# Smaller loads, a joint output step and shared evictions in the opening of an attention-and-MLP kernel

## The chip, the cores and the metric

One Trainium2 chip, one of its cores. The metric is the device time of one execution in microseconds (us). Three runs of the kernel before stand below. The profile is one further execution, whose own time and span are given beside it.

## The reference

Two parts are chained. The first is a decayed linear attention over batch 4, 8 heads, 768 positions and head size 64, in blocks of 64 positions with a running 64 by 64 state per batch and head. The second is an MLP without bias on all 3072 tokens: 512 to 2048, a quick GELU, 2048 to 512.

```
intra = einsum('bhic,bhjc->bhij', qb, kb) * Dmask          # lam**(i-j), i >= j
intra = einsum('bhij,bhjd->bhid', intra, vb)
inter = einsum('bhid,bhde->bhie', qb * lam_pow, kv_state)
out[:, :, sl] = intra + inter
kv_state = lam_block * kv_state + einsum('bhsd,bhse->bhde', kb * rev_pow, vb)
...
h = x @ w_in                                               # x: 3072 x 512, heads side by side
g = h * (1.0 / (1.0 + np.exp(-1.702 * h)))
return g @ w_out
```

Inputs and output are float32; the kernel multiplies in bfloat16 and accumulates in float32.

## The kernel before, in words

The 3072 tokens are worked in six waves of 512. Waves 0 and 1 are the first 256 positions of two batches each (the "big" form); waves 2 to 5 take 128 positions of all four batches. Heads go in four pairs; pair p holds heads 2p and 2p+1. The MLP of a wave begins once the attention output x of all four pairs is there: `mlp1` makes 16 tiles of 512 columns, each of four accumulating steps kc 0 to 3, and kc p reads x of pair p. `mlp2` makes four output tiles of 16 steps each.

The order of every instruction on every engine is written out by hand (`manual_schedule`), and an engine works in that order. Wave 0's attention is a straight list of calls in the opening. The attention of wave w + 1 is slipped between the MLP's items of wave w: `BIG` lists for wave 1 at which item each step is placed, and `EARLY = 3` is the number of `mlp1` tiles that are begun on pairs 0 and 1 before the output step of pairs 2 and 3.

The steps of the big form, for one pair p:

- `big_cast` (L225) multiplies k or q by powers of lam into `kqb`, one instruction per batch, on VectorE (`V`) or GpSimd (`G_`). `big_cast_v` (L229) casts v on GpSimd.
- `big_t` (L238) transposes k and q on TensorE into PSUM and evicts them to `kqB`: ACT (L242), or for q VectorE (L240).
- `big_s` (L255) makes the scores in two PSUM banks, `big_m` (L262) masks and scales them on VectorE into `sm`, a tile with six buffers.
- `big_kv` (L279) makes the products of k and v of two pairs for both halves of the 256 positions. ACT copies the first half into `mid` (L283) and into `first` (L284). `big_st` (L291) joins the halves into the state `kv` for wave 2, on VectorE.
- `big_c` (L299, L307) makes the output of one pair from `mid`, v and the masked scores. Two PSUM banks are evicted to x (L311), by ACT or by VectorE.

`fill` (L217) puts matmuls on zeros into the order, which write a bank that the next step overwrites. PSUM banks come from two pools: five for attention, three for transposes of wave 0 and for the MLP.

Loads of q, k and v are issued by SP (the first two of q by ACT). The weights `w_in` (five column tiles) and `w_out` (four) are issued by GpSimd (L176, L180), in between its casts. A small load that reads w_out (`sync_behind_weights`, L188) holds SP's next loads, those of wave 1, back until a part of the weights has landed.

## Time and profile before

| what | value |
|---|---|
| runs | 304.63, 215.71, 215.8 us; median 215.8 |
| profiled execution | 215.14 us, span 213.4 us |
| granted TensorE clock | 0.999 |
| TensorE (PE) busy | 204.8 us, 96% of the span |
| VectorE (DVE) busy | 83.8 us, 39% |
| ScalarE (ACT) busy | 87.4 us, 41% |
| GpSimd (POOL) busy | 33.2 us, 16% |
| DMA | 33.83 MB, 159 GB/s over the span |

A busy time is the sum of the engine's instruction durations without overlap. A large share says that the engine is nearly always at work; where the idle rest lies must be read from stretches of the span. In rows of the timeline and of the chain of waits the first number is the start and the second the length, both in us; square brackets hold the idle time before a group and what ended it.

### The profile page before, as it was taken

The page shows a single profiled execution, that of the slowest core. Times are in us where ns is not written, and L with a number is a line of the kernel's source. Part 1 is how long each engine was busy: PE and PEld are TensorE (multiplying, and loading weights), DVE is VectorE, ACT ScalarE, POOL GpSimd, SP SyncE. Part 2 cuts the span into 40 slices and gives each one's busy share as a digit, 9 for nine tenths or more (in the row PEclk, how much of TensorE's full clock was granted, in tenths as well). Part 3 has the DMA queues.
Part 4 walks back from the last instruction along what each step waited for, and adds up shares of the span by engine and source line. Part 5 has one row for each costly group of instructions (what it writes and reads, how often), then busy time and mean ns, then how long its engine had stood idle before and what let it go on. Part 6 is the DMA issues. An engine that isn't in the chain of part 4 may idle for free.

```text
span 213.4 us, 4323 instructions
## 1 busy us (share of the span) xinstructions
PE 204.8 (96%) x1757; PEld 101.1 (47%) x1757; DVE 83.8 (39%) x186; ACT 87.4 (41%) x164; POOL 33.2 (16%) x62
## 2 busy tenths in 40 slices
PE   7779999999999999999999999999999999999994
PEld 2454444545444455444545444545444545444453
DVE  3687100285751573624272624272624071100121
ACT  4683673445666122366302366302376302466000
POOL 4599000562130012101110001120000000000000
PEclk9999999999999999999999999999999999999999
DMA  5999999999899989699981399981390012100112
GB/s 137 268 248 198 203 197 248 295 267 200 186 276 213 198 190 229 221 188 223 221 195 52 114 184 223 227 191 56 114 178 0 3 51 94 53 2 0 49 49 98
DMA packets 88839, 33.83 MB, mean 159 GB/s; under 512 B 68724, under 2 KB 85876, under 8 KB 88820
## 3 DMA queue, kind: packets, MB, share of 16 engines
q1 hardware_dynamic: 83524, 29.11, 57.9%
q0 software_dynamic: 4752, 4.19, 12.5%
q10 hardware_dynamic: 544, 0.26, 0.5%
q8 instruction: 13, 0.21, 0.4%
q14 instruction: 6, 0.05, 0.1%
HBM read 27.27 MB, written 6.29 MB: 157 GB/s over the span
## 4 chain that ended last, share of the span: by engine, by line
PE 91%; DMA 4%; DVE 1%; ACT 1%; POOL 1%; SPq 0%; issue 0%; POOLq 0%
PE ps_h L378 39%; PE ps_out L391 38%; DMA vb<-in_v_dram 2%; PE ps_o L362 2%; PE ps_o L355 2%; PE ps_s L321 2%; PE ps_part L402 2%; DMA qb<-in_q_dram 2%; PE ps_o L307 1%; PE ps_s L255 1%; PE ps_kv L279 1%; PE ps_kv L338 1%; ACT xT L311 1%; PE ps_tq L238 1%; ACT g_sb L381 1%; POOL vb L229 1%
## 5 line engine op out<-in xcount | busy, mean ns | idle before, releaser
L378 PE MATMUL ps_h<-xT,w_in 128*128 128x512 bf16 x384 | 85.3, 379 | 1.1 <-ACT xT L311 0.5
L391 PE MATMUL ps_out<-w_out,g_sb 128*128 128x512 bf16 x368 | 83.7, 379 | 0.0
L381 ACT ACTIVATE g_sb<-ps_h 128x512 bf16<-128x512 f32 x96 | 56.9, 597 | 44.9 <-PE ps_h L378 44.6
L378 PEld LDWEIGHTS <-w_in 128*128 128x128 bf16 x384 | 37.0, 98 | 45.5 <-issue 1.6
L391 PEld LDWEIGHTS <-g_sb 128*128 128x128 bf16 x368 | 34.5, 98 | 40.2
L325 DVE SCALAR_TENSOR_TENSOR sm<-ps_s,inv_pow,mask 128x512 bf16<-128x512 f32 x32 | 21.8, 744 | 28.6 <-PE ps_s L321 28.6
L395 DVE COPY o_sb<-ps_out 128x512 f32<-128x512 f32 x19 | 13.1, 691 | 47.0 <-PE ps_out L391 46.6
L367 ACT CAST xT<-ps_o 128x512 bf16<-128x512 f32 x16 | 8.6, 589 | 44.4 <-PE ps_o L362 44.4
L202 POOL CAST v_sb<-vf 128x512 bf16<-128x512 f32 x16 | 10.4, 652 | 84.8 <-DMA vf<-in_v_dram 84.8
L225 DVE TENSOR_TENSOR kqb<-kb,kb_pow 128x256 bf16<-128x256 f32 x14 | 6.3, 492 | 19.7 <-DMA kb<-in_k_dram 17.1
L262 DVE SCALAR_TENSOR_TENSOR smb<-ps_s,inv_pow,mask_b 128x512 bf16<-128x512 f32 x16 | 11.0, 745 | 5.9 <-PE ps_s L255 4.8
L345 DVE SCALAR_TENSOR_TENSOR kv<-kv,blk_pow,ps_kv 128x256 bf16<-128x256 bf16 x12 | 5.2, 478 | 17.2 <-PE ps_kv L338 17.2
L200 DVE TENSOR_SCALAR kqs<-qf,q_pow 128x256 bf16<-128x256 f32 x32 | 11.1, 348 | 0.6 <-DMA qf<-in_q_dram 0.6
L225 POOL TENSOR_TENSOR kqb<-qb,qb_pow 128x256 bf16<-128x256 f32 x12 | 7.8, 663 | 22.0 <-DMA qb<-in_q_dram 19.7
L199 DVE TENSOR_SCALAR kqs<-kf,k_pow 128x256 bf16<-128x256 f32 x32 | 11.1, 347 | 0.0
L395 ACT COPY o_sb<-ps_out 128x512 f32<-128x512 f32 x4 | 2.3, 585 | 10.4 <-PE ps_out L391 10.4
L242 ACT COPY kqB<-ps_tk 128x512 bf16<-128x512 bf16 x8 | 4.6, 594 | 2.5 <-PE ps_tk L238 2.4
L238 PEld LDWEIGHTS <-kqb 128*128 128x128 bf16 x64 | 3.9, 98 | 3.6 <-DVE kqb L225 1.3
L355 PEld LDWEIGHTS <-kv 64*64 64x64 bf16 x128 | 3.8, 106 | 3.4 <-issue 3.4
L217 PE MATMUL fill<-warm 128*128 128x512 bf16 x10 | 4.0, 584 | 1.3 <-DVE i_blk L135 1.3
L321 PEld LDWEIGHTS <-kqT 64*128 64x128 bf16 x128 | 3.6, 94 | 3.4 <-issue 3.4
L229 POOL CAST vb<-vb 128x512 bf16<-128x512 f32 x8 | 4.7, 616 | 3.3 <-DMA vb<-in_v_dram 3.2
(61 smaller groups left out, 99.5 us busy)
## 6 DMA issues: line engine op xcount, KB each, us to landing
out_dram<-o_sb SPq DMA_DIRECT2D x23, 256.0 KB, 2.0
kf<-in_k_dram SPq DMA_DIRECT2D x32, 128.0 KB, 3.3
qf<-in_q_dram SPq DMA_DIRECT2D x32, 128.0 KB, 3.5
vf<-in_v_dram SPq DMA_DIRECT2D x32, 128.0 KB, 3.4
vb<-in_v_dram SPq DMA_DIRECT2D x8, 256.0 KB, 5.2
w_out<-in_moe_w_out_dram POOLq DMA_DIRECT2D x4, 512.0 KB, 14.2
kb<-in_k_dram SPq DMA_DIRECT2D x6, 256.0 KB, 5.5
qb<-in_q_dram SPq DMA_DIRECT2D x6, 256.0 KB, 5.9
```

The lines of the kernel that those rows point to most:

```text
L199: nc.vector.tensor_scalar(ks[:, :, h, :], kf[:, :, h, :], scalar1=k_pow[:, hd : hd + 1], scalar2=None, op0=MUL)
L200: nc.vector.tensor_scalar(qs[:, :, h, :], qf[:, :, h, :], scalar1=q_pow[:, hd : hd + 1], scalar2=None, op0=MUL)
L202: nc.gpsimd.tensor_copy(v_sb[w % 2][p], vf)
L225: eng.tensor_tensor(x[:, bb].rearrange("p t (h d) -> p h t d", h=2), pair_of(w, nm, p)[:, bb], by, op=MUL)
L262: nc.vector.scalar_tensor_tensor(sm.rearrange("p b t s -> p b (t s)"), s2.rearrange("p b t s -> p b (t s)"), inv_pow[:, 2 * p + h : 2 * p ...
L325: nc.vector.scalar_tensor_tensor(sm, s2[p, h], inv_pow[:, 2 * p + h : 2 * p + h + 1], mask.to_broadcast([P, B, P]), op0=MUL, op1=MUL)
L355: nc.tensor.matmul(ps_o[p][hs, b, :], kv_sb[w % 2][p][hs, b, :], trans[w, p][hs, 1, b, :], start=(b == 0), stop=False, skip_group_check=True)
L367: nc.scalar.copy(x, ps_o[p].rearrange("p b s -> p (b s)"))
L378: nc.tensor.matmul(h_ps[fc], w_in_sb[j][:, kc, i * P : (i + 1) * P], xT[w, kc], start=(kc == 0), stop=(kc == KC - 1))
L381: nc.scalar.activation(g_of[w][:, fc, :], h_ps.pop(fc), GELU)
L391: nc.tensor.matmul(ps_out, g_of[w][:, fc, g * P : (g + 1) * P], w_out_sb[j][:, fc % CW, :], start=(fc == 0), stop=(fc == FFC - 1))
L395: (nc.scalar.copy if w == 0 else nc.vector.tensor_copy)(o, ps_out)
```

## The change

- Wave 0 loads k and q of pairs 2 and 3 pair by pair (k2, q2, k3, q3), 128 KB a load, where it loaded 256 KB for both; v of these pairs comes last, as before.
- `big_cast` takes one engine per batch: the q products of wave 0's pairs 1 to 3 are made half on GpSimd, half on VectorE.
- `big_t` can do k or q alone, so the transposes of pairs 2 and 3 are spread between other steps.
- `big_c` takes a tuple of pairs. Pairs 0 and 1 are one step with two PSUM banks and one copy per bank; x of two pairs is one tile. Each bank is evicted by its own engine, ACT and VectorE in most places; in wave 0 the joint step's copies are both on ACT and placed later (`big_x`).
- `big_parts` has ACT copy both halves of the k and v products to SBUF in float32 (`part`), and `big_st` joins them on GpSimd with two instructions per pair, after wave 0's weights have been issued.
- `sm` has eight buffers.
- `mlp1`'s early tiles run [0, 1] and then [2, 3], where they ran [0, 1], [2], [3].
- `BIG` is renumbered, with wave 1's transposes and scores of pairs 0, 1 one item later; other engines take some of its casts.
- The third and later w_in tiles move behind later casts on GpSimd, and the fillers of wave 0 are fewer.

```diff
-        for nm, h0 in (("v", 0), ("k", 4), ("q", 4), ("v", 4)):
-            load_big(0, nm, h0, 4, nc.sync)
+        load_big(0, "v", 0, 4, nc.sync)
+        for h0 in (4, 6):
+            for nm in "kq":
+                load_big(0, nm, h0, 2, nc.sync)
+        load_big(0, "v", 4, 4, nc.sync)
...
-    def big_cast(w, nm, p, eng):
+    def big_cast(w, nm, p, *engs):
...
-        for bb in range(BB):
+        for bb, eng in enumerate(engs if len(engs) == BB else engs * BB):
...
-        for h in range(2):
+        for h, eng in enumerate(engs):
             hs = slice(64 * h, 64 * h + 64)
-            nc.scalar.copy(mid_sb[p0 // 2][hs, :, :, hs], ps_kv[0][hs])
-        nc.scalar.copy(first_sb[p0 // 2], ps_kv[0])
-        kv_of[w, p0] = ps_kv[1]
+            eng(mid_sb[p0 // 2][hs, :, :, hs], ps_kv[0][hs])
+        kv_of[w, p0] = ps_kv
+        if parts:
+            big_parts(w, p0)
+
+    def big_parts(w, p0):
+        for r, ps_kv in enumerate(kv_of.pop((w, p0))):
+            nc.scalar.copy(part_sb[p0 // 2][r], ps_kv)
 
     def big_st(w, p0):
...
-            nc.vector.scalar_tensor_tensor(kv_sb[0][p][:, BB * w : BB * w + BB], first_sb[p0 // 2][:, i],
-                                           blk_pow[:, p : p + 1], ps_kv[:, i], op0=MUL, op1=ADD)
+            nc.gpsimd.tensor_scalar(part_sb[p0 // 2][0][:, i], part_sb[p0 // 2][0][:, i], scalar1=blk_pow[:, p : p + 1],
+                                    scalar2=None, op0=MUL)
+            nc.gpsimd.tensor_tensor(kv_sb[0][p][:, BB * w : BB * w + BB], part_sb[p0 // 2][0][:, i],
+                                    part_sb[p0 // 2][1][:, i], op=ADD)
...
+    def big_c(w, pairs, fills=0, evict=(nc.scalar.copy, nc.vector.tensor_copy)):
+        n, p0 = len(pairs), pairs[0] // 2 * 2
+        ps_o = [bank([P, n, BB, 2, D], f32, f"ps_o{r}") for r in range(2)]
...
+        c_of[w, pairs] = x_of[w, p0][:, pairs[0] % 2 : pairs[0] % 2 + n], ps_o
+        for r, eng in enumerate(evict):
+            big_x(w, pairs, r, eng)
...
-    BIG = [(27, big_cast, "k", 0, V), (27, big_cast, "q", 0, G_), (27, big_cast, "k", 1, V), (27, big_cast, "q", 1, G_),
-           (27, big_cast_v, 0), (27, big_cast_v, 1), (30, big_t, 0), (31, big_t, 1), (31, big_s, 0), (31, big_m, 0),
...
+    BIG = [(24, big_cast, "k", 0, V), (24, big_cast, "q", 0, G_), (24, big_cast, "k", 1, V), (24, big_cast, "q", 1, G_),
+           (24, big_cast_v, 0), (24, big_cast_v, 1), (24, big_cast, "k", 2, G_), (28, big_t, 0), (29, big_t, 1),
+           (29, big_s, 0), (29, big_m, 0), (30, big_s, 1), (30, big_m, 1), (30, big_cast, "k", 3, V),
+           (30, big_cast, "q", 2, G_), (30, big_cast, "q", 3, G_, V), (31, big_kv, 0, False), (32, big_c, (0, 1)),
...
-        return ([(mlp1, w, fc, kcs) for kcs in ([0, 1], [2], [3]) for fc in range(EARLY)]
+        return ([(mlp1, w, fc, kcs) for kcs in ([0, 1], [2, 3]) for fc in range(EARLY)]
...
         load_w_in(0)
+        big_kv(0, 0, False, 3, parts=False)
+        big_cast(0, "k", 2, V)
+        big_t(0, 2, "k")
+        big_c(0, (0, 1), 3, ())
+        big_cast(0, "q", 2, G_, V)
         load_w_in(1)
-        big_kv(0, 0, False, 3)
-        big_cast(0, "k", 2, V)
-        big_c(0, 0, 8)
-        big_c(0, 1)
-        big_cast(0, "q", 2, G_)
-        load_w_in(2)
-        load_w_in(3)
-        big_cast(0, "k", 3, V)
-        big_cast(0, "q", 3, V)
-        big_st(0, 0)
-        big_t(0, 2, V)
-        big_t(0, 3, V)
-        big_s(0, 2, 2)
-        big_m(0, 2)
-        big_s(0, 3, 1)
+        big_cast(0, "k", 3, V)
+        big_parts(0, 0)
+        big_x(0, (0, 1), 0, nc.scalar.copy)
+        big_t(0, 2, "q", AV)
+        big_t(0, 3, "k")
+        big_cast(0, "q", 3, G_, V)
+        big_s(0, 2)
+        big_t(0, 3, "q")
+        big_x(0, (0, 1), 1, nc.scalar.copy)
+        big_m(0, 2)
+        load_w_in(2)
+        big_s(0, 3, 2)
         big_m(0, 3)
         big_cast_v(0, 2)
         big_cast_v(0, 3)
-        load_w_in(4)
+        for j in range(3, len(IN_COLS)):
+            load_w_in(j)
         for j in range(len(w_out_sb)):
             load_w_out(j)
+        big_kv(0, 2, False, 2)
         late_mask()
-        big_kv(0, 2, False)
...
```

More of the change, by code (lines that the diff above doesn't have):

```diff
@@ L164 @@
     kv_sb = [[const.tile([P, B, D], bf16, name=f"kv{i}{p}") for p in range(NP)] for i in range(2)]
-    first_sb = [const.tile([P, 2, BB, D], bf16, name=f"first{i}") for i in range(2)]
+    part_sb = [[const.tile([P, 2, BB, D], f32, name=f"part{i}{r}") for r in range(2)] for i in range(2)]
     mid_sb = [const.tile([P, 2, BB, P], bf16, name=f"mid{i}") for i in range(2)]
@@ L314, in scores, with big_x, x_tile @@
+    def big_x(w, pairs, r, eng):
+        x, ps_o = c_of[w, pairs]
+        eng(x.rearrange("p i (b r s t) -> p r (i b) t s", b=BB, r=2, t=2)[:, r],
+            ps_o[r].rearrange("p i b t s -> p (i b) t s"))
+    def x_tile(w, p0):
+        x = xp.tile([P, 2, W], bf16, tag=f"x{p0}", name="xT")
+        for i in range(2):
+            xT[w, p0 + i] = x[:, i]
+        return x
     def scores(w, pairs):
```

84 lines of the change are left out of this document (38 added, 46 removed).

## The prediction

> **What bounds the kernel now.** I read the page first, then stretches of time, then the chain of waits through the one stretch that is not full. The page:
>
> ```profile
> span 213.4 us, 4323 instructions
> ...
> PE 204.8 (96%) x1757; PEld 101.1 (47%) x1757; DVE 83.8 (39%) x186; ACT 87.4 (41%) x164; POOL 33.2 (16%) x62
> ```
>
> TensorE is busy for 96% of the span, so time can come only from the other 8.6 us and from its filler matmuls. Where they lie (columns: stretch, length, then each engine's busy time; last the granted clock, DMA share, GB/s):
>
> ```profile
> 1.25:22.67 21.42, 17.70 (x273) 9.39 (x274) 14.14 (x30) 12.94 (x32) 14.91 (x29) 1.00 1.06 225
> 23.00:34.00 11.00, 11.00 (x53) 5.00 (x51) 0.00 (x0) 7.76 (x14) 0.00 (x0) 1.00 1.23 200
> 54.00:58.00 4.00, 3.47 (x47) 1.79 (x46) 2.74 (x9) 2.26 (x6) 0.61 (x1) 1.00 0.96 215
> 57.85:208.00 150.15, 150.15 (x1105) 72.81 (x1105) 56.34 (x125) 55.49 (x95) 9.20 (x14) 1.00 0.59 135
> ```
>
> From 57.85 on TensorE has no gap before the tail, which the change leaves alone. Two places are left: the opening up to 22.67, and 0.53 us around 54 to 58, the entry into wave 1's MLP. The chain of waits through the opening (start, length, what):
>
> ```profile
> 10.34 1.18 POOL vb L229 x2
> ...
> 11.88 0.98 PE ps_o L217 x8
> ...
> 13.98 0.87 DVE kqb L225
> 14.85 0.52 DVE kv L291 x2
> 15.37 0.35 DVE kqB L240
> ...
> 16.57 0.40 PE ps_s L255 x16
> 16.98 0.75 DVE smb L262
> ...
> 18.21 1.46 PE ps_h L378 x6
> ```
>
> VectorE stands on it three times in a row at 13.98 (the q product of pair 3, two state updates, a q eviction): 1.74 us. The change takes two of these away. But a second runner is level with this chain; it shows as a wait in TensorE's weight loads (first row; then the DMA row of the second w_in tile, then GpSimd's issues):
>
> ```profile
> 19.05 0.11 PEld L378 LDWEIGHTS <-w_in 128*128 128x128 bf16 x2 [0.37 <-DMA w_in<-in_moe_w_in_dram]
> w_in<-in_moe_w_in_dram POOLq DMA_DIRECT2D x1, 256.0 KB, 6.6
> 11.45 1.68 POOL L176 DMA_DIRECT2D w_in<-in_moe_w_in_dram  x2
> ```
>
> The second w_in tile is issued in the later half of those 1.68 us, about 12.4, and lands 6.6 later, at 19.0; the third output tile of the MLP starts at 19.05. Whatever comes earlier ahead of it waits there, because TensorE runs in order and both output steps (pairs 2, 3) stand behind.
>
> **The change part by part.**
>
> *Smaller loads, shared q products, states off VectorE.* The rates:
>
> ```profile
> L225 DVE TENSOR_TENSOR kqb<-kb,kb_pow 128x256 bf16<-128x256 f32 x14 | 6.3, 492 | 19.7 <-DMA kb<-in_k_dram 17.1 <-ACT kb_pow L147 2.6
> L225 POOL TENSOR_TENSOR kqb<-qb,qb_pow 128x256 bf16<-128x256 f32 x12 | 7.8, 663 | 22.0 <-DMA qb<-in_q_dram 19.7 <-ACT qb_pow L147 2.3
> L242 ACT COPY kqB<-ps_tk 128x512 bf16<-128x512 bf16 x8 | 4.6, 594 | 2.5 <-PE ps_tk L238 2.4
> L311 ACT CAST xT<-ps_o 128x256 bf16<-128x256 f32 x12 | 4.3, 456 | 2.0 <-PE ps_o L307 2.0
> L291 DVE SCALAR_TENSOR_TENSOR kv<-first,blk_pow,ps_kv 128x128 bf16<-128x128 bf16 x8 | 2.4, 340 | 0.3 <-ACT first L284 0.3
> ```
>
> Up to 11.88 nothing moves: v of pairs 0, 1 ends that part as before. Then k of pair 2 is multiplied by about 12.3 and transposed while ACT fills `mid`; three fillers of 512 columns (0.7 us, at the 0.24 us per matmul of the 18.21 row) replace eight of 256 (0.98), and the joint step of 36 matmuls (1.1 us, what the chain has between the fillers' end at 12.86 and 13.98) ends near 14.2, 0.2 later than the two single ones. Now q of pair 2 and k of pair 3 wait ready, the q copy takes 0.35 on VectorE, and pair 2's scores start near 15.0 instead of 16.57. Pair 3's q takes its second half on VectorE behind that copy (0.5 to 0.9), an ACT copy (L242, 0.6), and its scores stand near 16.5. Four masks of 0.75 or a little less are then done near 18.4, not 19.7.
>
> The kv products of pairs 2, 3 next need v. Its last load now waits, in the program's order on SP's queue, for pair 2's k to land (each load waits for the one eight before it), so I put its issue at about 11.3 instead of 10.4. Today the casts start behind two weight issues:
>
> ```profile
> 14.51 1.55 POOL L176 DMA_DIRECT2D w_in<-in_moe_w_in_dram  x2
> 16.05 1.18 POOL L229 CAST vb<-vb 128x512 bf16<-128x512 f32 x2
> vb<-in_v_dram SPq DMA_DIRECT2D x2, 256.0 KB, 5.1
> ```
>
> In the new order only one weight issue stands ahead and the casts wait for v: 10.4 + 5.1 = 15.5 today, up to 16.4 with the later issue. Casts end at 16.7 to 17.6, kv near 17.1 to 17.9 instead of 18.21: 0.3 to 1.1 us gained at this point.
>
> *The weight gate.* On GpSimd the q product of pair 2 (0.66) now stands between the first and the second w_in issue, which moves from 12.4 to 13.05. If the landing is set by the issue it moves to 19.65; if by bytes (the DMA share of this opening is 1.06, full) it stays at 19.0. I take 19.15, nearer to the full queue's row. Two matmuls later (0.44), the output step of pair 2 starts at about 19.6 against 19.5 now. So the gain above is not collected: it ends in a longer wait for w_in. Term: +0.1 (bounds -0.8, if the gate opens early, to +0.6).
>
> *Two engines evict x, and the tiles run on.* Today ACT evicts both halves of pair 2, VectorE both of pair 3, and kc 2 and kc 3 are separate passes over three tiles; after the change each engine evicts one half of each pair and one pass does both. The two entries:
>
> ```profile
> 20.27 0.42 PE L307 MATMUL ps_o<-smb,vb 64*64 64x128 bf16 x16
> 20.96 1.46 PE L378 MATMUL ps_h<-xT,w_in 128*128 128x512 bf16 x6 [0.27 <-ACT xT L311]
> 55.45 0.42 PE L307 MATMUL ps_o<-smb,vb 64*64 64x128 bf16 x16
> 57.85 10.52 PE L378 MATMUL ps_h<-xT,w_in 128*128 128x512 bf16 x48 [0.25 <-ACT g_sb L381]
> L381 ACT ACTIVATE g_sb<-ps_h 128x512 bf16<-128x512 f32 x96 | 56.9, 597 | 44.9 <-PE ps_h L378 44.6
> ```
>
> The last output matmul ends at 20.69 and at 55.87; the MLP runs free at 22.67 (20.96 + 1.46 + 0.25) and 57.85: 1.98 us both times, of which six matmuls are 1.3 (48 in 10.52). In the new form x of pair 3 is ready 0.5 after the step (one 0.46 copy on each engine); the first tile's kc 3 ends at 0.72, the other two tiles at 1.58. The first GELU (0.6, some 0.2 after its last matmul) ends then too, so its bank is free: 1.58 instead of 1.98. Term: -0.4 in wave 0 and -0.4 in wave 1 (bounds 0, if a copy waits behind another, to -0.6 each).
>
> *Costed at nothing.* Eight mask buffers: the third pair's masks start at 16.98, after the step that read the first pair's ended at 13.98, so six never made anyone wait; without that cover one mask, 0.75. States on GpSimd: eight instructions a wave, none of which the trace shows; between the two nearest rows, 0.34 (L291, as wide, on VectorE) and 0.66 (L225, twice as wide, on GpSimd), they last 2.7 to 5.3 us. In wave 0 they follow the weight issues, and GpSimd does nothing from 23 to 34 (the second stretch above); in wave 1 they push the v casts of wave 2, which are first needed at 74.78. Without that cover: up to 5 us in wave 1. The second ACT copy of a part (under 0.46, L311) falls between `mid` and the x copies. Wave 1's first transposes stand one group of four matmuls (0.87) later; today they just meet q (and the row of the v casts' first use):
>
> ```profile
> 40.51 1.75 POOL L225 TENSOR_TENSOR kqb<-qb,qb_pow 128x256 bf16<-128x256 f32 x3 [0.21 <-DMA qb<-in_q_dram]
> 41.02 0.44 PE L238 MATMUL ps_tq<-ident,kqb 128*128 128x128 bf16 x4
> 74.78 0.57 PE ps_o L362 x16
> ```
>
> TensorE arrives 0.3 earlier and 0.87 later, so q may be 0.5 late for free; beyond that TensorE waits, at most 1.0 by the bound on the weights.
>
> **Sum.** +0.1 - 0.4 - 0.4 = -0.7. The profiled execution took 215.14 for a span of 213.4; it becomes 214.4 for 212.7. The median of the runs shown is 215.8, 0.7 above the profiled execution; the prediction on that scale is 215.1.
>
> **The rivals.**
>
> *The gate opens early.* w_in lands before the earlier kv work needs it, and the opening also keeps 0.8 of what VectorE gave up. For: smaller loads finish sooner. Against: TensorE already waits 0.05 at 19.05, and the issue is later. -0.8 - 0.8 = -1.6: 214.2.
>
> *v and the weights collide (slower).* Both queues in one stretch, 13 to 16:
>
> ```profile
> q0 software_dynamic: 634, 0.32, 87.1%
> q1 hardware_dynamic: 615, 0.30, 38.0%
> ```
>
> Alone q1 moved 0.30 MB in 38% of 3 us, 0.26 MB per us. If the throttled last v loads (0.5 MB) still have to move when weights start at 13.5, and get half the engines' time (the rows leave them less), they need 3.8 us and land near 17.3, not 15.5. Casts end at 18.5, kv near 18.9, pair 2's output step starts at 20.4: +0.9. The three later w_in issues and all of w_out, queued behind those casts on GpSimd, slip by up to 3, and wave 1's inputs behind them: +0.6 more. +0.9 + 0.6 - 0.8 = +0.7: 216.5. It decides once v lands after 16.4. The Trainium skill, DMA: Bandwidth & Descriptors, DMA queue model, says that each DMA engine takes turns between the queues with work, packet by packet; by that rule an even share holds, and with it 216.5 once the bytes are late. The shares of this stretch, 87.1% for the weights, agree so far; whether the bytes are late no run here shows.
>
> *Nothing gets through.* The freer entry meets the next tile's weights or wave 1's q, and both terms are given back: 215.8.
>
> **How the numbers follow.** Forecast 0.5; gate early 0.2; collision 0.2; nothing 0.1. The range takes 214.2 to 216.5 and a little on either side for the unknown prices: 213.9 to 216.6. Over 2% (4.3 us), about what a measurement of this kernel can tell from no change, needs more than any case here: faster 0.02, since all idle time from 1.25 to 57.85 is 3.7 + 0.5 = 4.2; slower 0.03; within 0.95.
>
> **What would show it.** Right: pair 2's scores near 15.0, a weight-load wait for w_in well above 0.37 just before pair 2's output step, that step still at 19.4 to 19.8, and 1.6 us from the last output matmul to a free MLP in both waves. Wrong: that step before 19.0 (gate early) or after 20 (collision), v casts after 16.5, or a TensorE gap at wave 1's transposes.

## The result, and the profile after

| kernel | median | ratio to the kernel before, 95% interval | profiled execution |
|---|---|---|---|
| before | 215.76 us (22 runs) | 1 | 215.14 us, span 213.4 |
| changed | 216.84 us (22 runs) | 1.0053 [1.003, 1.0076] | 216.09 us, span 214.4 |

The ratio and its interval are worked out from the fast executions of both kernels timed side by side, and are not the quotient of the two medians. The change makes the kernel slower by half a per cent, 1.1 us. Forecast were 215.1 us and a gain of 0.7. First the page of the changed kernel, then stretches of it (length, then busy time of TensorE, its weight loads, VectorE, ScalarE, GpSimd; clock, DMA share, GB/s):

```profile
span 214.4 us, 4303 instructions
...
PE 202.6 (94%) x1726; PEld 101.0 (47%) x1753; DVE 85.0 (40%) x178; ACT 89.0 (42%) x164; POOL 41.4 (19%) x78
```

```profile
1.25:22.67 21.42, 17.82 (x267) 9.43 (x271) 13.67 (x26) 14.50 (x33) 14.51 (x29) 1.00 1.03 215
23.00:34.00 11.00, 10.95 (x51) 4.99 (x52) 0.00 (x0) 7.65 (x14) 3.87 (x8) 1.00 1.22 195
39.00:46.00 7.00, 6.14 (x68) 3.17 (x66) 2.70 (x6) 3.41 (x6) 4.47 (x8) 1.00 1.05 283
...
68.00:70.00 2.00, 1.70 (x21) 0.78 (x21) 0.95 (x2) 1.00 (x2) 0.00 (x0) 1.00 0.97 190
```

The last two stretches in the kernel before:

```profile
39.00:46.00 7.00, 7.00 (x74) 3.57 (x71) 3.66 (x8) 3.22 (x6) 5.43 (x10) 1.00 1.17 289
68.00:70.00 2.00, 2.00 (x24) 1.00 (x23) 1.21 (x2) 0.81 (x3) 0.00 (x0) 1.00 1.07 198
```

TensorE had no gap in either of them and now has 0.86 and 0.30. TensorE's own rows there, changed kernel (start, length; in brackets the wait before it and what ended it):

```profile
42.10 0.28 PE L243 MATMUL ps_tq<-ident,kqb 128*128 128x128 bf16 x2 [0.24 <-POOL kqb L228]
42.84 0.28 PE L243 MATMUL ps_tq<-ident,kqb 128*128 128x128 bf16 x2 [0.46 <-POOL kqb L228]
...
69.21 0.40 PE L343 MATMUL ps_s<-kqT 64*128 64x128 bf16 x8 [0.25 <-DMA kqT<-kqs]
```

These are wave 1's first transposes of q and wave 2's first scores. In the kernel before the same scores start without a wait, at 68.31, the very time at which the second of their two tiles of transposed k and q (`kqT`) lands by the trace's DMA records:

```profile
68.31 0.62 PE L321 MATMUL ps_s<-kqT 64*128 64x128 bf16 x16
```

The second half of these 16 matmuls reads that tile and starts at 68.54, by the single instructions of the trace. So this place had a slack of 0.2 us, and a page without a wait did not show how little that is. The changed kernel's chain of waits tells where the lateness comes from (start, length, what):

```profile
10.63 6.09 DMA vb<-in_v_dram
...
16.85 1.16 POOL vb L232 x2
18.01 1.43 POOL w_in L179 x2
19.44 0.13 POOL w_out L183
...
20.16 13.45 DMA w_out<-in_moe_w_out_dram
...
33.62 0.75 SPq L191
...
35.94 6.16 DMA qb<-in_q_dram
...
42.17 0.62 POOL kqb L228
```

Read it downwards: v's last load takes 6.09 us, GpSimd casts it, and only then issues two w_in tiles and w_out; the second w_out tile lands at 33.61, the small load behind the weights lets SP go on, and wave 1's second load of q lands at 42.10. In the kernel before no load of weights stands on the chain up to 45 us. GpSimd's rows, changed kernel:

```profile
16.85 1.16 POOL L232 CAST vb<-vb 128x512 bf16<-128x512 f32 x2 [1.86 <-DMA vb<-in_v_dram]
17.96 1.48 POOL L179 DMA_DIRECT2D w_in<-in_moe_w_in_dram  x2
19.42 2.98 POOL L183 DMA_DIRECT2D w_out<-in_moe_w_out_dram  x4
```

Before, w_in's fourth tile was issued at 15.31, the fifth at 17.16, and w_out from 17.89 on. So w_in's fourth tile moved by 2.65, because the change puts it behind the casts. Of the 1.53 by which w_out moved, 0.80 come from the casts, which start at 16.85 and not at 16.05, and 0.73 from that one issue more ahead of it. The later loads moved with them; the table of landings below has the times.

The ledger, from the starts of TensorE's groups in the two timelines:

| part | before | changed | difference | forecast |
|---|---|---|---|---|
| start of pair 2's output step, wave 0 | 19.50 | 19.62 | +0.12 | +0.1 |
| from there to the first `mlp2` (33.90, 33.70) | 14.40 | 14.08 | -0.32 | -0.4 |
| to wave 1's products of k and v, pairs 2, 3 (53.00, 53.56) | 19.10 | 19.86 | +0.76 | 0 |
| to wave 2's first scores (68.31, 68.56) | 15.31 | 15.00 | -0.31 | -0.4 |
| to the last half tile (206.63, 207.30) | 138.32 | 138.74 | +0.42 | 0 |
| from there to the end of the span | 6.80 | 7.06 | +0.26 | 0 |
| sum | 213.43 | 214.36 | +0.93 | -0.7 |

Both gains that were forecast are there within 0.1. The loss stands in three rows that were forecast as zero.

This ledger is of one execution of each kernel. Other profiled runs have the same instructions up to pair 2's output step. With the changed opening (the runs below with states on VectorE, with the old entry, with the places later and with less for the DMA to do) that step starts at 19.21, 19.79, 20.02 and 20.46; with the opening of the kernel before (new entry with old and with later places, only the places moved, less for the DMA to do) at 19.52, 18.84, 19.04 and 18.88. With the two of the ledger the means are 19.82 and 19.16. So the changed opening is probably later by more than the 0.12 of the first row.

TensorE's granted clock is 1.00 in all the stretches above, but not in every execution. Ten of the changed kernel's 22 runs had a mean clock of 0.989 to 0.992; their median is 217.0 us, that of the other twelve 216.45. Of the 151 runs of the kernel before that were timed beside the experiments below, four had a mean clock this low. By these medians 0.7 of the 1.1 us remain where the clock did not fall. The last section shows such a fall.

### The profile page after: what moved, and what is told of

Its sections match the earlier page's. It is cut to its first block, busy times and chain, and to the rows that moved or that the text cites. A ratio compares the mean times of both kernels' runs of the same rounds, so it can differ in the third digit from the quotient of the medians.

```text
span 214.4 us, 4303 instructions
## 1 busy us (share of the span) xinstructions
PE 202.6 (94%) x1726; PEld 101.0 (47%) x1753; DVE 85.0 (40%) x178; ACT 89.0 (42%) x164; POOL 41.4 (19%) x78
## 4 chain that ended last, share of the span: by engine, by line
PE 75%; DMA 17%; SPq 2%; issue 2%; POOL 2%; DVE 0%; POOLq 0%
PE ps_out L412 33%; PE ps_h L399 31%; DMA w_out<-in_moe_w_out_dram 6%; DMA qb<-in_q_dram 5%; DMA vb<-in_v_dram 3%; PE ps_o L384 2%; PE ps_o L377 2%; PE ps_s L343 2%; DMA kb<-in_k_dram 2%; DMA kqT<-kqs 2%; PE ps_part L423 2%; SPq L96 1%; PE ps_kv L360 1%; POOL w_in L179 1%; PE ps_o L316 1%
## 5 line engine op out<-in xcount | busy, mean ns | idle before, releaser
L412 PE MATMUL ps_out<-w_out,g_sb 128*128 128x512 bf16 x352 | 81.0, 379 | 1.7 <-issue 1.4
L228 DVE TENSOR_TENSOR kqb<-kb,kb_pow 128x256 bf16<-128x256 f32 x14 | 7.6, 581 | 21.8 <-DMA kb<-in_k_dram 19.1
L203 DVE TENSOR_SCALAR kqs<-qf,q_pow 128x256 bf16<-128x256 f32 x32 | 12.0, 374 | 0.7 <-DMA qf<-in_q_dram 0.7
L202 DVE TENSOR_SCALAR kqs<-kf,k_pow 128x256 bf16<-128x256 f32 x32 | 11.8, 369 | 0.0
L228 POOL TENSOR_TENSOR kqb<-qb,qb_pow 128x256 bf16<-128x256 f32 x12 | 8.0, 680 | 17.6 <-DMA qb<-in_q_dram 15.1
L343 PE MATMUL ps_s<-kqT 64*128 64x128 bf16 x128 | 5.1, 217 | 0.4 <-DMA kqT<-kqs 0.2
L296 POOL TENSOR_SCALAR part<-part,blk_pow 128x128 f32<-128x128 f32 x8 | 4.9, 609 | 2.7 <-ACT part L291 2.7
```

Of the source, the lines that this page charges most:

```text
L202: nc.vector.tensor_scalar(ks[:, :, h, :], kf[:, :, h, :], scalar1=k_pow[:, hd : hd + 1], scalar2=None, op0=MUL)
L203: nc.vector.tensor_scalar(qs[:, :, h, :], qf[:, :, h, :], scalar1=q_pow[:, hd : hd + 1], scalar2=None, op0=MUL)
L228: eng.tensor_tensor(x[:, bb].rearrange("p t (h d) -> p h t d", h=2), pair_of(w, nm, p)[:, bb], by, op=MUL)
L343: nc.tensor.matmul(s2[p, h][:, b, :], kq[hs, 0, b, :], kq[hs, 1, b, :], start=True, stop=True)
L412: nc.tensor.matmul(ps_out, g_of[w][:, fc, g * P : (g + 1) * P], w_out_sb[j][:, fc % CW, :], start=(fc == 0), stop=(fc == FFC - 1))
```

## The experiments

The main theory (A in the first expectations): the change puts the stream of loads back, and since weights, wave 1's and wave 2's inputs run level with TensorE up to some 70 us, every gain in computing is given back as a wait at the two places above. The rivals put the loss on an engine (GpSimd's states, the casts, the new entry) or on a later opening. "Places" below are wave 1's transposes and scores of pairs 0, 1 and wave 2's first scores.

First the trace's landing times and waits of the runs that the argument needs (us; each from one profiled execution, ratios from the timed runs):

| | before | changed | weights first | changed, less DMA | entry, old places | entry, later places | changed, later places |
|---|---|---|---|---|---|---|---|
| last v load of wave 0 lands | 15.45 | 16.72 | 17.37 | 16.02 | 15.36 | 14.82 | 17.12 |
| second w_out tile lands | 31.89 | 33.61 | 32.74 | 30.36 | 32.93 | 31.79 | 33.84 |
| wave 1's second q load lands | 40.44 | 42.10 | 42.30 | 39.12 | 41.91 | 40.28 | 42.33 |
| second `kqT` of wave 2 lands | 68.31 | 69.16 | 70.25 | 66.68 | 69.25 | 67.55 | 70.40 |
| first `mlp2` of wave 0 | 33.90 | 33.70 | 34.38 | 34.55 | 33.60 | 32.92 | 34.10 |
| wait at wave 1's q | 0 | 0.70 | 0.38 | 0 | 1.46 | 0 | 0 |
| wait at wave 2's scores | 0 | 0.25 | 0.96 | 0 | 0 | 0 | 0.75 |
| this execution's time | 215.14 | 216.09 | 217.18 | 215.62 | 216.42 | 214.21 | 215.81 |
| median of the timed runs | 215.76 | 216.84 | 216.78 | 214.6 | 215.57 | 214.34 | 214.92 |
| ratio | 1 | 1.0053 | 1.0022 | 0.9968 | 0.9999 | 0.9954 | 0.996 |

Only the ratios compare kernels: each was timed beside the kernel before, whose median in these comparisons lay between 215.3 and 215.97. A profiled execution lies up to 1.3 from its kernel's median, so its landings and waits are an instance and not a mean. With one and the same opening, the second w_out tile landed between 31.50 and 32.93 in four executions.

### One part of the change undone at a time

Weights first: the fourth and fifth w_in tile ahead of the casts that wait for v.

```diff
+        for j in range(3, len(IN_COLS)):
+            load_w_in(j)
         big_cast_v(0, 2)
         big_cast_v(0, 3)
-        for j in range(3, len(IN_COLS)):
-            load_w_in(j)
```

> The changed kernel with the fourth and fifth w_in tile issued before GpSimd's casts of v of pairs 2 and 3, not after. Theory A (late weights): in the changed kernel GpSimd waits for v until 16.85 and issues the rest of the weights from 17.96 on, so w_out's second tile lands at 33.6 instead of 31.9, wave 1's inputs 1.7 later, and TensorE stands 0.7 us at wave 1's q transposes and 0.4 at wave 2's first scores. With this edit w_in 4 is issued near 15.0, w_out's second tile lands near 32, both stalls go, and the time is 1.0 to 1.2 below the changed kernel: about 215.2 to 215.8 on the scale of medians, at or a little under the kernel before. Rival B (the states on GpSimd slow VectorE's casts of wave 2): the wave 1 stall may go, but the stall at wave 2's scores stays: 0.6 below the changed kernel. Rival C (the later place of wave 1's transposes): no gain, 216.8.

Measured: 1.0022 [0.9994, 1.005]. Against 1.0053 that is 0.7 us in the theory's direction, a third short or more, and the two intervals overlap, so this run alone does not show a gain. In the profiled execution w_out lands 0.9 earlier, but v lands at 17.37, the opening is 0.7 later, and wave 2's scores wait:

```profile
70.30 0.40 PE L343 MATMUL ps_s<-kqT 64*128 64x128 bf16 x8 [0.96 <-DMA kqT<-kqs]
```

Whole loads: k and q of pairs 2, 3 in 256 KB again.

```diff
-        for h0 in (4, 6):
-            for nm in "kq":
-                load_big(0, nm, h0, 2, nc.sync)
-        load_big(0, "v", 4, 4, nc.sync)
+        for nm in "kqv":
+            load_big(0, nm, 4, 4, nc.sync)
```

> The changed kernel with k and q of pairs 2 and 3 loaded together again (256 KB a load, v last). Theory A1 (v is late because its last load waits for one eight before it and then shares the engines with weights): v lands near 15.5 instead of 16.7, the later weights are issued about 1.1 earlier, at 16.8, and most of the 0.7 stall of wave 1 goes; the opening is 0 to 0.5 later because pair 2's q comes later. Span 0.4 to 0.9 below the changed kernel. Rival A2 (v is late only because the first weights start at 12.9 instead of 13.5): v still lands after 16.3 and the span does not fall, or rises by the opening's loss.

Measured: 1.0042 [1.0014, 1.007]. That is within the changed kernel's interval; the gain of 0.4 to 0.9 is not there. In the profiled execution v lands at 15.62, but the v of pairs 0 and 1, whose casts stand ahead of the first w_in issue, lands at 10.85 and not at 9.65; that issue comes at 12.10 and not at 10.89, and w_out's second tile lands at 33.89. One delay of the stream is exchanged for another. The opening is later too (first `mlp2` at 34.98), and some of that can be the granted clock, which was 0.70 and 0.73 from 12 to 15 and from 15 to 18 us.

States on VectorE, in one instruction each:

```diff
-            nc.gpsimd.tensor_scalar(part..., scalar1=blk_pow..., op0=MUL)
-            nc.gpsimd.tensor_tensor(kv..., part..., part..., op=ADD)
+            nc.vector.scalar_tensor_tensor(kv..., part..., blk_pow..., part..., op0=MUL, op1=ADD)
```

> The changed kernel with the states joined on VectorE again, one instruction a pair, from the same two copied parts. Theory A: the states on GpSimd stand where nothing waits, so the time stays within 0.2 of the changed kernel (216.8) and the 0.7 stall at wave 1's q stays. Rival B (GpSimd's state instructions slow VectorE's casts of wave 2, and with them the transposes by DMA): the stall of 0.4 at wave 2's first scores goes and the time falls by 0.4.

Measured: 1.0038 [1.0013, 1.0063], within the changed kernel's interval. The profiled execution waited 1.9 at wave 1's q with no state left on GpSimd. The states are not the cause.

The old entry: one engine evicts both halves of a pair, kc 2 and kc 3 in separate passes, and the list of wave 1 renumbered to match.

```diff
+        if len(pairs) == 1 and evict:
+            evict = (nc.scalar.copy, nc.scalar.copy) if pairs[0] == 2 else (nc.vector.tensor_copy, nc.vector.tensor_copy)
...
-        return ([(mlp1, w, fc, kcs) for kcs in ([0, 1], [2, 3]) for fc in range(EARLY)]
+        return ([(mlp1, w, fc, kcs) for kcs in ([0, 1], [2], [3]) for fc in range(EARLY)]
```

> The changed kernel with the old way into the MLP: x of pair 2 evicted by ACT alone, of pair 3 by VectorE alone, and the early tiles in three passes [0, 1], [2], [3]; the places of wave 1's steps moved by three so that they stand where they stood. Theory A: the entry is worth 0.3 to 0.4 in each wave (1.98 us from the last output matmul to a free MLP instead of 1.6); in wave 0 that loss is taken up by the wait for q in wave 1, so only wave 1's shows and part of that goes into the wait at wave 2's scores: 0 to 0.4 above the changed kernel. If the entry is worth nothing: same time and the same 1.6 us.

Measured: 1.0058 [1.0031, 1.0085], so in the changed kernel the new entry is worth nothing that can be measured, though the ledger shows its 0.3 in both waves. That what it gains is given back behind it fits the theory.

### Less for the DMA to do

Both kernels without the load of the fifth w_in tile (512 KB); the matmuls read the fourth tile instead.

```diff
-    in_of = [(j, i) for j, c in enumerate(IN_COLS) for i in range(c)]
+    in_of = [(min(j, 3), i) for j, c in enumerate(IN_COLS) for i in range(c)]
```

> The changed kernel without the load of its fifth w_in tile (512 KB, some 2.5 us of the DMA stream); the matmuls that used its columns read the fourth tile instead, so the products of a quarter of the hidden columns are others, and every engine's instructions and their order are the same. Theory DMA (the stream of weights and of wave 1's and wave 2's loads runs level with TensorE, and the change put it 0.9 to 1.7 us back): w_out, the load behind the weights and wave 1's loads land some 2 us earlier, TensorE's wait at wave 1's transposes of q (0.70 us now) and at wave 2's first scores (0.25 to 0.4) goes, and the time is 0.7 to 1.1 below the changed kernel: 215.7 to 216.1. Rival, engines (wave 1's casts on GpSimd and its transposes one item later make q late, and GpSimd's states slow the casts of wave 2): the waits stay, and the time is that of the changed kernel within 0.3.

> The kernel before, without the load of its fifth w_in tile in the same way (the matmuls read the fourth tile instead). Theory DMA: the kernel before has no wait of TensorE at wave 1's q or wave 2's scores, so an earlier stream gives it nothing: within 0.3 of the kernel before, and the changed kernel without that load is as fast or faster than this one, by up to 0.6. Rival (the kernel before is held by its DMA stream as well, somewhere that its trace doesn't show): 0.5 or more below the kernel before.

Measured: the changed kernel falls from 1.0053 to 0.9968 [0.9947, 0.9988], 1.8 us; the kernel before to 0.9977 [0.9954, 1.0], 0.5 us. Both waits are gone from the changed kernel's trace. This execution began `mlp2` 0.85 later than the changed kernel's, with a granted clock of 0.62 from 12 to 15 and 0.81 from 15 to 18 us, which by itself shortens waits for loads; but q lands 2.98 earlier and the second `kqT` 2.48 earlier, more than the waits. All instructions but the one issue are the same, in the same order, on the same engines: what changed is the stream. The gain exceeds the 0.7 to 1.1 expected. For the kernel before the theory expected at most 0.3 and its rival 0.5 or more: by the ratio the rival is nearer, though the interval reaches 1.0. Without the tile the two kernels are level, 0.9968 and 0.9977.

### The entry alone, the places alone

The kernel before with the new entry, first with wave 1's and wave 2's steps later, then at their old places (counted from the end of the list); and the kernel before with only the places moved.

```diff
-            (x_out or nc.scalar.copy)(x..., ps_o[r])
+            (x_out or (nc.scalar.copy, nc.scalar.copy))[r](x..., ps_o[r])
...
-        return ([(mlp1, w, fc, kcs) for kcs in ([0, 1], [2], [3]) for fc in range(EARLY)]
+        return ([(mlp1, w, fc, kcs) for kcs in ([0, 1], [2, 3]) for fc in range(EARLY)]
...
+                    late = 2 if w == 1 and i == 0 else 0
-                    side += [(n + SCORES_AT[i] + at, (scores, w + 1, ps2)), ...]
+                    side += [(n + SCORES_AT[i] + at + late, (scores, w + 1, ps2)), ...]
```

> The kernel before with its opening as it was and only the MLP's entry of the change: the last output steps of waves 0 and 1 evict one bank on ACT and one on VectorE, the early tiles run pairs 0, 1 and then 2, 3 together; wave 1's transposes and scores of pairs 0, 1 one item later and wave 2's first scores two items later, so that an MLP that begins earlier does not come upon loads that are not there. Theory DMA (the entry's gain of 0.3 to 0.4 in each wave was real and was given back as waits for loads, since the opening put the stream back): 0.4 to 0.8 below the kernel before, 215.0 to 215.4. Rival (the entry's gain is given back whatever the stream does, by an engine): within 0.2 of the kernel before.

> The kernel before with the new entry, but wave 1's transposes and scores and wave 2's first scores at the places where the kernel before has them. Theory level stream (q of wave 1 and the transposed k and q of wave 2 come at the very time at which the kernel before uses them): TensorE waits some 0.4 more at wave 1's q and some 0.4 at wave 2's first scores, and a half or more of the entry's gain is given back: 0.997 to 0.9995 of the kernel before. Rival (the loads come earlier with the computing, since their buffers do): 0.9954 as with the later places.

> The kernel before with its own opening and its own entry, and only the places moved: wave 1's transposes and scores of pairs 0 and 1 one item later, wave 2's first scores two items later. It completes a table of four: old entry and old places (the kernel before), new entry and old places (0.9999), new entry and later places (0.9954). Theory (the kernel before waits at those places little or not at all, the places are worth something only to a kernel whose MLP begins earlier): 0.9985 to 1.0005. Rival (the later places are the gain, the entry is worth nothing by itself): 0.9955 to 0.997.

And the changed kernel, opening and entry untouched, with the places moved:

```diff
-            ... (28, big_t, 0), (29, big_t, 1), (29, big_s, 0), ... (30, big_s, 1), ... (32, big_c, (0, 1)),
+            ... (29, big_t, 0), (30, big_t, 1), (30, big_s, 0), ... (31, big_s, 1), ... (33, big_c, (0, 1)),
```

> The changed kernel with its opening and its entries as they are, and only three places moved: wave 1's transposes and scores of pairs 0 and 1 one item of the MLP later, their output step one later, and wave 2's first scores two items later. Theory level stream (the changed kernel loses its gains as waits for loads at wave 1's q, 0.7, and at wave 2's scores, 0.25 to 0.4): these waits go and the time is 0.7 to 1.1 below the changed kernel, 0.9995 to 1.002 of the kernel before. Rival (the opening is later in most executions than in the profiled one, and the places are a small part): 1.003 to 1.005.

| | places as they were | places later |
|---|---|---|
| kernel before | 1 | 0.997 [0.9948, 0.9992] |
| its opening, new entry | 0.9999 [0.9972, 1.0025] | 0.9954 [0.9924, 0.9983] |
| changed kernel (new opening, new entry) | 1.0053 [1.003, 1.0076] | 0.996 [0.9934, 0.9986] |

This shows where the loss stands. With later places the changed kernel comes from 1.0053 to 0.996: 0.9%, 2.0 us, with no edit to its opening, its loads or its engines, and it is then level with the kernel before at later places (0.997). That is more than both waits of its profiled execution (0.95), and more than expected; the rival with 1.003 to 1.005 fell.

Two things it does not show. The places are worth 0.3% even to the kernel before, whose profiled execution does not wait there; the theory expected 0.9985 to 1.0005 for that run, and the rival's 0.9955 to 0.997 came. Waits in other executions than the profiled one would explain it, and no run shows them. And the entry by itself has no gain that these runs can tell from none: 0.9999 where the places stay, 0.9954 against 0.997 where they are later, with intervals that overlap. Its 0.3 in each wave is shown by the traces alone.

The new entry with old places waits for q in its profiled execution, in the same words as the changed kernel:

```profile
41.86 0.28 PE L238 MATMUL ps_tq<-ident,kqb 128*128 128x128 bf16 x2 [0.96 <-POOL kqb L225]
42.64 0.28 PE L238 MATMUL ps_tq<-ident,kqb 128*128 128x128 bf16 x2 [0.50 <-POOL kqb L225]
```

With later places the chain of waits of its profiled execution from 9 to 45 us has no DMA in it at all, and from 20.61 on TensorE is nearly all of it; four of its pieces:

```profile
20.61 1.68 PE ps_h L378 x7
22.34 10.74 PE ps_h L378 x49
...
33.35 7.50 PE ps_out L391 x34
40.85 0.22 PE ps_tk L238 x4
```

The rival that the loads would come earlier with the computing, 0.9954 with old places too, has 0.9999 against it. The execution with old places begins `mlp2` 0.30 earlier than the kernel before, and its q lands 1.47 later; most of that is the spread of the stream, since w_out's second tile was issued only 0.16 later and landed 1.04 later.

### Repairs of the opening

Weights first, and wave 2's first scores two items later:

> The changed kernel with the fourth and fifth w_in tile issued ahead of the casts of v of pairs 2 and 3 (as in the run with the weights first), and wave 2's first scores two items of the MLP later (0.85 us each). Theory DMA: in the run with the weights first wave 2's scores waited 1.0 us for the transposed k and q; two items later they are there, the wait goes and the time is 0.5 to 1.0 below that run: 215.8 to 216.3. Rival, engines: the wait turns up at the next step that needs the scores (wave 2's mixing), and the time is that of the run with the weights first.

Measured: 1.0 [0.9978, 1.0023], no wait at wave 2's scores; between the run with weights first and the changed kernel with all places later, as the theory has it, with intervals that overlap both.

That kernel with the first w_in tile behind GpSimd's half of pair 2's q product:

```diff
-        load_w_in(0)
         big_kv(0, 0, False, 3, parts=False)
...
         big_cast(0, "q", 2, G_, V)
+        load_w_in(0)
         load_w_in(1)
```

> The changed kernel with its weights ahead of the second casts of v and wave 2's first scores later (the run that came to 1.000 of the kernel before), and with the first w_in tile issued behind GpSimd's half of pair 2's q product, together with the second: some 1.3 us after the last load of v and not 0.2 to 0.3. Theory collision (v of pairs 2 and 3 is stretched in some executions since the weights start right behind it, and this keeps the opening 1 us behind that of the kernel before): v lands 4.3 to 5.2 us after its issue, near 15.0 to 15.6, and the time is 0.4 to 1.0 below that run, 0.9955 to 0.998 of the kernel before. Rival (the opening is held by the products and their evictions, not by v): no change, 1.000; where the first w_in tile itself becomes late, above it.

Measured: 0.9988 [0.9962, 1.0015]. v landed 3.7 to 3.9 us after its issue, sooner even than the collision theory's 4.3 to 5.2, but the time can't be told from 1.0. Not settled by this run.

The new entry with later places, plus the smaller loads:

> The kernel before with the new entry and the later steps of waves 1 and 2 (the run that came to 0.9954 of the kernel before), and of the change's opening only the loads: k and q of pairs 2 and 3 come pair by pair, 128 KB each. Nothing of wave 0's computing moves. Theory collision: SP needs some 1 us for the two more issues, less what the smaller loads land earlier, v of pairs 2 and 3 is issued 0.3 to 0.7 later and lands later, in some executions over 16: 0.2 to 0.8 above that run, 0.9965 to 0.999. Rival (the smaller loads cost nothing, the opening's other edits do): 0.9954 within 0.001.

Measured: 1.0011 [0.9983, 1.0038] against 0.9954 [0.9924, 0.9983]: by the ratios the smaller loads alone cost 1.2 us, more than the 0.2 to 0.8 expected, and the intervals touch. In the profiled execution not for the reason expected: v lands at 15.68, not over 16. VectorE's queue, four products of k, with whole loads and then with small ones:

```profile
11.32 1.42 DVE L225 TENSOR_TENSOR kqb<-kb,kb_pow 128x256 bf16<-128x256 f32 x4
```

```profile
11.40 3.11 DVE L228 TENSOR_TENSOR kqb<-kb,kb_pow 128x256 bf16<-128x256 f32 x4
```

With small loads each of the four takes some 0.83 us instead of 0.41, with no idle time between them: k of pair 3 was in at 12.38, and its first product starts at 12.90. So VectorE was slow there, and not waiting for k. The last two run beside products of GpSimd, the first two beside its weight issues; why the first two are slow is open, since in the kernel before a product beside such an issue took 0.42. The first `mlp2` is 0.93 later than with whole loads, but only 0.25 later than in the other run with whole loads and the new entry (old places). How much the smaller loads cost by themselves this run does not tell. The opposite edit, whole loads in the changed opening with weights first and later scores:

> The changed kernel with its weights ahead of the second casts of v and wave 2's first scores later (the run that came to 1.000), and with k and q of pairs 2 and 3 in whole loads of 256 KB as in the kernel before. Theory small loads (the smaller loads alone cost 1.2 in the kernel before with the new entry, since v of pairs 2 and 3 is issued and lands later and the weights' stream with it): 0.5 to 1.0 below that run, 0.9955 to 0.998. Rival (in the changed opening, whose products and transposes were set for the smaller loads, whole loads make pair 2 late by as much as v comes earlier): 1.000 within 0.002.

Measured: 0.9974 [0.9955, 0.9994] against 1.0 [0.9978, 1.0023]: 0.6 us, the lower end of the theory, but the intervals overlap.

Last, the two best versions with an earlier stream: the changed kernel with all three repairs, and the kernel before with new entry, later places and the fifth w_in tile ahead of the casts.

> The changed kernel with the three places of waves 1 and 2 later (that alone came to 0.996), the weights ahead of the second casts of v, and the first w_in tile behind GpSimd's half of pair 2's q product. Theory level stream: with the later places TensorE waits little for the stream (0.8 at wave 2's scores in the profiled execution of that run), so an earlier stream is worth at most that: 0.993 to 0.996. Rival (weights ahead of the casts make the opening itself later, since the casts of v and with them pair 2's output step wait for GpSimd): 0.997 to 0.999.

> The kernel before with the new entry and the later places (0.9954), and the fifth w_in tile issued ahead of the casts of v of pairs 2 and 3, not behind them. Its profiled execution has no wait for a load past the opening, so by the theory an earlier stream is worth little: 0.993 to 0.996. Rival (the casts of v and the opening become 0.7 later, by one issue of GpSimd): 0.997 to 0.999.

Measured: 0.997 [0.9945, 0.9995] and 0.9976 [0.9952, 0.9999]. Nothing is gained over 0.996 and 0.9954. Both ratios lie in their rivals' range and not in the theory's, though all these intervals overlap; an earlier stream has no gain that can be seen once TensorE comes later to the two places. The lowest ratio of all is that of the kernel before with its own opening, the new entry and later places: 0.9954, with a median of 214.34 us where the kernel before took 215.49 beside it. Against the kernel before that is a gain; against the other versions with later places, 0.996 and 0.997, it can't be told.

## Why the prediction was wrong

The smaller loads, and what VectorE gave up: right in the time, with luck. Pair 2's scores start at 14.90 (forecast near 15.0), but the part ahead of them, of which the text says "nothing moves", ended at 11.32 and not at 11.88, since v of pairs 0 and 1 landed 0.56 earlier; from there the scores took 3.6 where the text has 3.1. Casts of v were forecast to end at 16.7 to 17.6; they end at 18.01, because v's last load landed at 16.72 and not by 16.4. It was issued at 10.63, earlier than the forecast 11.3, and took 6.1 us instead of 5.1. kv ends its wait for them:

```profile
14.90 0.42 PE L256 MATMUL ps_s<-kqB 64*64 64x128 bf16 x16
...
18.06 0.32 PE L280 MATMUL ps_kv<-vb,kqb 64*64 64x64 bf16 x16 [0.24 <-POOL vb L232]
18.31 0.98 PEld L399 LDWEIGHTS <-w_in 128*128 128x128 bf16 x6
...
19.62 0.28 PE L307 MATMUL ps_o<-kqB,mid 128*128 128x128 bf16 x2
```

The weight gate: right number, wrong reason. Pair 2's output step starts at 19.62 (forecast 19.6), but the gate had opened: the first two w_in tiles landed at 17.01 and 18.34, 0.67 earlier than before, and TensorE's loads of w_in (18.31, above) have no wait. What held the step was v. In the other executions with the changed opening the step lay between 19.21 and 20.46, so the term of +0.1 is also too small by the means above, +0.7. A step can be hit by two errors that cancel, and only the row that names the releaser shows it.

The entry: right mechanism, size 0.31 and 0.32 instead of 0.4. The rows, wave 0 and wave 1 (last output matmuls, first tile, free run):

```profile
20.39 0.42 PE L316 MATMUL ps_o<-smb,vb 64*64 64x128 bf16 x16
20.82 0.39 PE L399 MATMUL ps_h<-xT,w_in 128*128 128x512 bf16 x1
21.39 1.69 PE L399 MATMUL ps_h<-xT,w_in 128*128 128x512 bf16 x7 [0.17 <-DVE xT L327]
```

```profile
56.02 0.42 PE L316 MATMUL ps_o<-smb,vb 64*64 64x128 bf16 x16
56.46 0.39 PE L399 MATMUL ps_h<-xT,w_in 128*128 128x512 bf16 x1
57.02 3.19 PE L399 MATMUL ps_h<-xT,w_in 128*128 128x512 bf16 x13 [0.17 <-DVE xT L327]
```

Costed at nothing: this is the step that failed. The text says of wave 1's q that it "may be 0.5 late for free; beyond that TensorE waits, at most 1.0 by the bound on the weights". The condition was right and its price was left out of the sum; nor does the 1.0 follow from that bound, 0.6, which leaves a wait of 0.1. The sum priced the second w_in tile alone, while the change had put w_in's fourth tile and one issue more ahead of w_out behind the casts of v. Wave 1's load of q was 1.7 late (42.10 for 40.44), and that part cost 0.76. The same reasoning was not carried on to wave 2, where a gap of zero was read as "no gap before the tail, which the change leaves alone"; it cost 0.42. And the tail, which the text takes as left alone, became 0.26 longer. Two of the text's own signs of being wrong came, v casts after 16.5 (16.85) and a TensorE gap at wave 1's transposes (0.70). A sum in which the first term makes TensorE earlier must ask of each later load whether it comes earlier too; here none did.

GpSimd's states (0.61 and 0.45 us, between the bounds 0.34 and 0.66) and the eight mask buffers cost nothing, as forecast.

The rival in which v and the weights collide had the right chain. Its condition was met: v landed after 16.4, later w_in and w_out slipped behind the casts (by 2.65 for w_in's fourth tile, 1.53 for w_out's first; "by up to 3" was forecast, for three w_in issues where two stand behind the casts), and wave 1's inputs with them. It named +0.6 for wave 1, measured 0.76, and its 216.5 is near the 216.84. Its other half, pair 2's output step at 20.4 with v at 17.3, did not come in this execution (19.62, v at 16.72); in the run with the places later, which has the same opening, v landed at 17.12 and the step started at 20.02. The Trainium skill, DMA: Bandwidth & Descriptors, Queues, rings and completion order (arbitration), has the DMA engines take turns between the queues packet by packet, and an even share would have put v near 17.3. By packets and bytes the two queues were near even from 13 to 16 (634 and 615, 0.32 and 0.30 MB), by time they were not (87.1% and 38.0%). Landings at 14.74 and 17.37 in two kernels with the same opening neither bear out the rule of turns nor speak against it; they show that no fixed price follows from it.

## What to carry to other kernels

Before a stage that computes earlier is priced, list for each later use of a load when it lands against when it is used: where the two lie close, as at 68.31 and 68.54 here, the profile shows no wait and there is next to no slack, and the gain stops there. A load that is issued by an engine with other work stands behind that engine's waits: an order that put two w_in tiles behind the casts of a late v moved all of w_out and, behind it, the inputs of the next two waves. Where the stream can't be made earlier, move the use later: a few numbers in a list were worth 0.9% to the changed kernel, more than the whole change had cost. And the same move on the kernel before belongs beside it: it gained 0.3% there, so not all of the 0.9% is loss of the change undone.

## What the runs showed of the hardware

The same load took very different times. The run with weights first and the run with weights first and later scores have the same opening; v's two loads, time from issue to landing, min, median and max, in the first and in the second:

```profile
DMA to landing us min/median/max: 6.6/6.6/6.7
```

```profile
DMA to landing us min/median/max: 4.0/4.2/4.3
```

What decides it was not found; the weights' first issue came 0.23 to 0.30 after v's last one in both.

TensorE's granted clock fell to a half for 3.41 us in three profiled executions of the changed kernel's variants, by the trace's clock records. Its row on their pages (40 equal slices of the span, tenths of full speed), whole loads, less for the DMA to do, states on VectorE:

```profile
PEclk9979999999999999999999999999999999999999
PEclk9969999999999999999999999999999999999999
PEclk9999999969999999999999999999999999999999
```

The first two begin in the opening, at 13.19 and 12.75 us; the third at 44.61, 1.0 after TensorE's wait of 1.66 for wave 1's q. A matmul that takes 0.216 us at other times (output step, 64x128) takes 0.311 in such a stretch. Runs with a mean clock this low are ten of the changed kernel's 22 and 29 of the 120 of its ten variants, against one of 60 among the five variants with the opening and the loads of the kernel before. The changed opening has fewer fillers and other waits; which of them makes the clock fall was not tried.

A product shared by two engines is not made in half the time. Changed kernel, GpSimd and then VectorE, halves of q and others:

```profile
11.89 0.84 POOL L228 TENSOR_TENSOR kqb<-qb,qb_pow 128x256 bf16<-128x256 f32 x1
...
45.12 1.18 POOL L228 TENSOR_TENSOR kqb<-kb,kb_pow 128x256 bf16<-128x256 f32 x2
```

```profile
12.18 0.83 DVE L228 TENSOR_TENSOR kqb<-qb,qb_pow 128x256 bf16<-128x256 f32 x1
...
14.78 0.41 DVE L228 TENSOR_TENSOR kqb<-qb,qb_pow 128x256 bf16<-128x256 f32 x1
```

Side by side the halves take 0.84 and 0.83; apart, 0.59 on GpSimd and 0.41 on VectorE. The Trainium skill, SBUF — State Buffer, Who interferes with whom, says that a product of two tensors on VectorE with both inputs in SBUF contends with what GpSimd reads; these rows agree. Not every pair loses on both sides: with the new entry and old places, VectorE's product at 13.84 took 0.41 beside one of GpSimd that took 0.85.

The end of the program became 0.26 longer, with every engine done. After the last store SP passes through nine semaphore waits, about 0.06 us each:

```
              last store lands   waits of SP done   of nine waits, behind the landing
before             212.47            212.57                   2
changed            213.14            213.49                   6
```

The wait that the last store ends stands eighth in one program and fourth in the other, and the rest follow it one by one. From the start of the last half tile to the end of the span, the changed kernel and its eight variants with small loads took 7.04 to 7.07, its two with whole loads 6.81. The kernel before and its two variants with the old entry took 6.80 to 6.82, the three with the new entry 6.92 to 6.94, and 7.17 where the smaller loads came to it. So the smaller loads, four more of them, go with a wait four places earlier and with 0.24 to 0.25 more at the end, in the three pairs that differ by them.
